# Attention and mixture of experts on one core: batch 0's values ahead of the next keys at the start, and the table filled from another tile

## The chip, the cores and the metric

The kernel runs on one core of a Trainium2 chip. The core has a matrix engine (TensorE, "PE" in the profile), a vector engine (VectorE, "DVE"), an activation engine (ScalarE, "ACT"), a general engine (GpSimd, "POOL") and a sync engine ("SP"), whose queue issues the loads and stores. Each engine works through its own instructions in order and waits on semaphores. The metric is device time in microseconds, lower is better, as the median of several executions.

## The reference

```python
# q, k, v: batch 8, heads 8, sequence 576, head size 64
k_p = k.reshape(B, H, Sp, 8, D).mean(axis=3)      # Sp = 72
v_p = v.reshape(B, H, Sp, 8, D).mean(axis=3)
scores = scale * np.matmul(q, k_p.transpose(0, 1, 3, 2))
attn = np.exp(scores - np.max(scores, axis=-1, keepdims=True))
attn = attn / (np.sum(attn, axis=-1, keepdims=True) + 1e-09)
x = np.matmul(attn, v_p)                          # then (4608 tokens, 512)
# experts: tokens with x @ w_skip > 0 go to the argmax of x @ w_gate
h = np.maximum(xc[mask] @ w1[e], 0.0)
y[mask] = gate_w[mask, None] * (h @ w2[e])
out[do_compute] = xc + y
```

Keys and values are averaged over groups of 8 rows, so that each query sees 72 of them. The 4608 tokens then go through 8 experts with 512 and 1024 columns, each token through one or none.

## The kernel before

`attention` goes over 36 tiles of 128 tokens (line 632, `for t in range(NT)`). A batch is 576 tokens, 4.5 tiles. For one tile the steps are: scores of two halves of the heads (TensorE, line 296), the minima of the negated scores (VectorE, line 303, tile `nm`), eight exponentials (ScalarE, line 310, `e`), six transposes (TensorE, lines 321 and 325) with two copies (ScalarE, lines 322 and 326), the product with the values (TensorE, line 339, two tiles or more later), and the normalisation and store (VectorE and SP, lines 356 to 364). `LAG = 4`: tile t's loop pass does the scores of t, the exponentials of t - 1, the transposes of t - 2 and the values of t - 4. Three PSUM buffers hold score halves, so a half needs the buffer of the half three before it.

A batch's keys are loaded into `stage` (`load_k`, line 187), summed over 8 by VectorE in four groups (line 209, tile `kp`) and written by ScalarE into a block-diagonal tile `kbd` (line 212). A batch's values are loaded into `hlo` or `hhi`, with a small remainder in `vl` (`load_v`, line 215), and summed over 8 (`pool_v`, lines 230 to 232, tiles `vs` and `ls`): on VectorE for batch 0, on POOL for the rest. TensorE transposes the sums (line 255), ScalarE copies them (`vT`), TensorE multiplies them with the gate columns (line 264), ScalarE copies these (`gs`), and two products (lines 273 and 276) put them beside the values in `vbd` and `vl4`.

The order on PE, ACT and DVE is that of the program's text (`manual_schedule`, line 154). It is set by generators that are stepped in the loop: `extra` (line 609) steps the key sums, `sums` (line 627) steps the value sums, and lines 682 to 691 start a batch's values or load the next. SP issues in the order of the text, with at most eight transfers under way before it waits for the one eight back. POOL's order is made by a scheduler that follows the dependencies.

Before the loop (lines 585 to 602) three matmuls on the tile `init` warm TensorE, and the loads go out: keys 0, the queries of tiles 0 and 1, the identity, the queries of tiles 2 and 3, values 0, keys 1, constants. `table` (in memory, 36,864 rows of two numbers) is filled with a marker from `init`, whose memory is later the ring of token tiles, and which is therefore cleared a second time (lines 448 and 449).

Of the kernel before, what the change touches and what calls it, by code (L numbers as in the profile page):

```python
# [26 lines left out]
F32 = mybir.dt.float32  # L27
# [12 lines left out]
NTOK = B * S  # L40
# [66 lines left out]
def emit(tc, q, k, vm, vr, wg, w1, w2, cf, out):  # L107
    nc = tc.nc
    with ExitStack() as top:
# [13 lines left out]
        rows = cp.tile([SLOTS, 256], F32, name="rows")  # L123
# [37 lines left out]
def attention(tc, nc, q, k, vm, vr, cf, w1, w2, whi, wlo, out, c, pay, offs, table, load_constants, near, bufs, late, early, fin):  # L161
    with ExitStack() as ctx:
# [10 lines left out]
        init = early("ring", 128, F)  # L173
        nc.gpsimd.memset(init, NO_TOKEN)
# [12 lines left out]
        def load_k(b, part=0):  # L187
            n = 4 * SP * POOL
            kt = flat(stage)[:, b % 2 * n:b % 2 * n + n].rearrange("p (g k i) -> p g k i", g=4, i=POOL)
            if part:  # L190
                for g in (range(0, 1) if part == 1 else range(1, 4)):
                    nc.sync.dma_start(kt[:, g], k[b, :, g])
            else:
                nc.sync.dma_start(kt, k[b])
            return kt
# [26 lines left out]
        def pool_v(b, vt, vl):  # L222
# [49 lines left out]
            eng = nc.gpsimd if b else nc.vector  # L272
            eng.tensor_tensor(vb.rearrange("p g (h c) -> p g h c", h=2)[:, :, :, HD:VA - 1],
                                    gs[:, 0:72].rearrange("p (g h c) -> p g h c", g=4, h=2),
                                    pair.unsqueeze(3).broadcast_to([128, 4, 2, 9]), ALU.mult)
            eng.tensor_tensor(v4[:n, :, HD:VA - 1], gs[:n, 72:108].rearrange("p (g c) -> p g c", g=4),
# [3 lines left out]
        def load_q(i, part=0, qt=None):  # L280
            s = 128, QG, 4, 128
            qt = qt or (qp.tile(list(s), F32, name="qt") if i % 3 == 2 else early("xlo" if i % 3 else "xhi", *s))
            sl = (slice(None), slice(0, 1), slice(1, QG))[part]
            nc.sync.dma_start(qt[:, sl], q[i, :, sl])
            return qt
# [147 lines left out]
        def near_tokens():  # L433
# [14 lines left out]
            late("ring")  # L448
            nc.gpsimd.memset(bufs["ring"], 0.0)

# [141 lines left out]
        load_q(0, 2, qt[0])  # L592
        qt[1] = load_q(1)
        vt[0] = load_v(0)
        start_k(1)
        load_constants()
# [4 lines left out]
        nc.gpsimd.dma_start(table.rearrange("(p n) t -> p (n t)", p=128), init[:, 0:NE * NTOK * 2 // 128])  # L601
# [7 lines left out]
        def extra(budget):  # L609

            if kcur in kg and t > max(0, 4.5 * kcur - KAHEAD):
                next(kg[kcur], None)
                if kcur == 1:
                    next(kg[kcur], None)
                budget -= 7
            while budget > 0 and routes.step():
                budget -= 1
            if los and budget > 0:
                los.pop(0)[1]()
# [12 lines left out]
        for t in range(NT):  # L632
# [12 lines left out]
            if t > 0:  # L645
                es[t - 1] = exped(*sms.pop(t - 1))
# [30 lines left out]
            if t >= LAG:  # L677
                for _, b in parts(t - LAG):
                    if b in vgen:
                        finish(vgen.pop(b))  # L680
                os_[t - LAG] = values(t - LAG, *pts.pop(t - LAG))
            if nv < B and t >= max(3, 4.5 * nv + LAG - VAHEAD):
                vgen[nv] = pool_v(nv, *vt.pop(nv))
                next(vgen[nv])
                nv += 1
                if 1 < nv < B:
                    vt[nv] = load_v(nv)
            if t == 0:
                start_k(2)
            if t == 1:  # L690
                vt[1] = load_v(1)
# [94 lines left out]
def slots(tc, nc, c, offs, table, near, bufs, out, fin, p, psum):  # L786
# [50 lines left out]
    nc.gpsimd.indirect_dma_start(rows[:, :], None, table.rearrange("(r l) t -> r (l t)", l=128),  # L837
# [27 lines left out]
    rv = rows.rearrange("s (l t) -> s t l", t=2)  # L865
# [407 lines left out]
```

## Time and profile before

| | us |
|---|---|
| median of 3 runs | 561.47 (559.93 to 565.52) |
| the profiled execution | 559.05 |
| its span in the trace | 557.2 |
| mean granted TensorE clock | 0.978 |

The attention loop fills roughly the first 170 us of the span, and the experts the rest. A row of the trace's order of time gives start, duration, engine, line, operation, what it writes and reads, and in brackets the idle time before it and what ended that. In a row for a window the engines' busy times are followed by the granted clock, the busy share of the DMA engines and the GB/s that they moved. A row of transfers ends with the time from issue to landing.

### The profile page before, as it was taken

Reading aid. Unit: us, or ns where it says so; the run is one execution under the profiler, and the core shown is the slowest. Engines: PE = TensorE matmul, PEld = TensorE weight load, DVE = VectorE, ACT = ScalarE, POOL = GpSimd, SP = SyncE. Lnnn points to the kernel's source line nnn. Section 1 sums busy time; section 2 is a strip of 40 time slices with the busy share of each in tenths; the row PEclk is TensorE's granted clock in tenths of the full one; section 3 lists DMA queues with packets and bytes.
Section 4 is the critical chain, followed back from the end, with each engine's and each line's share of the span. In section 5 each row is a group of like instructions: output and inputs, shape, how many; then the busy total and the mean of one; then the engine's idle time right before and its main releaser. Section 6 shows DMA issues by size and latency. Waiting matters only on the chain. (4 is left out here: it accounts for less than half of the span.)

```text
span 557.2 us, 11058 instructions
## 1 busy us (share of the span) xinstructions
PE 509.7 (91%) x3346; PEld 456.0 (82%) x3347; DVE 296.6 (53%) x698; ACT 244.7 (44%) x671; POOL 215.4 (39%) x291
## 2 busy tenths in 40 slices
PE   7489999698898968999999999999999999999994
PEld 5389898587797848797989898998989898989893
DVE  3567777595767732224633563233254557565663
ACT  5459789488882112123422441222144445443441
POOL 3638628468963424120422042323232043304042
PEclk9689999799999999999999999999999999999998
DMA  8958879977992111014331533111243637462200
GB/s 292 383 226 319 293 269 224 332 247 170 285 235 80 23 38 49 22 59 172 115 125 56 169 129 103 57 38 54 75 169 121 244 108 268 157 239 101 95 27 7
DMA packets 33447, 86.03 MB, mean 154 GB/s; under 512 B 7485, under 2 KB 7746, under 8 KB 31488
## 3 DMA queue, kind: packets, MB, share of 16 engines
q1 hardware_dynamic: 25312, 71.62, 39.9%
q0 software_dynamic: 8096, 13.95, 7.7%
q8 instruction: 18, 0.29, 0.3%
q14 instruction: 21, 0.17, 0.1%
HBM read 73.79 MB, written 20.52 MB: 169 GB/s over the span
## 5 line engine op out<-in xcount | busy, mean ns | idle before, releaser
L1070 PE MATMUL psl<-xhi,w1hi 128*128 128x256 f32 (+3 forms) x416 | 122.0, 293 | 5.0 <-PEq L900 3.9
L1071 PE MATMUL psl<-xlo,w1hi 128*128 128x256 f32 (+3 forms) x416 | 121.3, 292 | 0.0
L1072 PE MATMUL psl<-xhi,w1lo 128*128 128x256 f32 (+3 forms) x416 | 121.3, 291 | 0.0
L1126 ACT ACTIVATE hhi<-psl 128x256 fp32r<-128x256 f32 (+4 forms) x104 | 41.9, 403 | 155.2 <-ACTq L900 154.2
L989 POOL DMA_INDIRECT out<-ring,slot x39 | 40.0, 1025 | 179.9 <-POOLq L900 172.5
L1085 PE MATMUL psf<-w2hi,hhi 128*128 128x512 f32 x240 | 96.1, 400 | 2.9 <-PEq L900 2.9
L1086 PE MATMUL psf<-w2lo,hhi 128*128 128x512 f32 x240 | 94.8, 395 | 0.0
L1183 DVE SCALAR_TENSOR_TENSOR hlo<-psl,hhi 128x256 fp32r<-128x256 f32 (+2 forms) x104 | 43.8, 423 | 79.0 <-DVEq L900 78.5
L1070 PEld LDWEIGHTS psl<-xhi,w1hi 128*128 128x128 f32 x416 | 78.1, 188 | 7.0 <-issue 6.4
L1088 PE MATMUL psf<-w2hi,hlo 128*128 128x512 f32 x200 | 79.1, 395 | 0.0
L1071 PEld LDWEIGHTS psl<-xlo,w1hi 128*128 128x128 f32 x416 | 78.2, 188 | 0.5
L1072 PEld LDWEIGHTS psl<-xhi,w1lo 128*128 128x128 f32 x416 | 78.1, 188 | 0.0
L310 ACT ACTIVATE e<-sc,nm 128x72 f32<-128x72 f32 x288 | 64.6, 347 | 11.8 <-DVE nm L303 11.5
L1172 DVE SCALAR_TENSOR_TENSOR ring<-psf,ring 128x512 f32 x25 | 18.8, 750 | 78.8 <-DVEq L900 78.8
L339 PE MATMUL o<-vbd,pT 128*128 128x148 f32 (+1 forms) x304 | 49.7, 300 | 9.8 <-DVE x L363 8.5
L1085 PEld LDWEIGHTS psf<-w2hi,hhi 128*128 128x128 f32 x240 | 45.1, 188 | 13.0 <-issue 3.3
L1086 PEld LDWEIGHTS psf<-w2lo,hhi 128*128 128x128 f32 x240 | 45.1, 188 | 9.7
L339 PEld LDWEIGHTS o<-vbd,pT 128*128 128x128 f32 (+1 forms) x304 | 41.2, 184 | 11.7 <-issue 9.1
L1135 ACT ACTIVATE xhi<-psd 128x512 fp32r<-128x512 f32 x36 | 18.9, 600 | 70.9 <-ACTq L900 70.9
L984 POOL DMA_INDIRECT ring<-out,slot x39 | 43.4, 1114 | 15.0 <-issue 12.5
L1088 PEld LDWEIGHTS psf<-w2hi,hlo 128*128 128x128 f32 x200 | 37.6, 188 | 9.1
L423 POOL DMA_INDIRECT table<-pay,r_di x36 | 35.6, 989 | 23.0 <-DVE rc L358 9.7
(220 smaller groups left out, 859.0 us busy)
## 6 DMA issues: line engine op xcount, KB each, us to landing
stage<-in_w SPq DMA_DIRECT2D x64, 512.0 KB, 4.4
out<-x SPq DMA_DIRECT2D x36, 256.0 KB, 5.7
stage<-in_k SPq DMA_DIRECT2D x7, 1152.0 KB, 8.9
hlo<-in_vm SPq DMA_DIRECT2D x4, 1024.0 KB, 9.8
hhi<-in_vm SPq DMA_DIRECT2D x4, 1024.0 KB, 7.0
xlo<-in_q SPq DMA_DIRECT2D x6, 512.0 KB, 6.6
qt<-in_q SPq DMA_DIRECT2D x6, 512.0 KB, 7.3
xhi<-in_q SPq DMA_DIRECT2D x5, 512.0 KB, 12.6
```

Of the source, the lines that this page charges most:

```text
L310: nc.scalar.activation(e[:, h, :], sc[h // 4][:, h % 4 * SP:(h % 4 + 1) * SP], AF.Exp, bias=nm[:, h:h + 1], scale=-1.0)
L339: nc.tensor.matmul(o_[sl, g * 2 * VA:(g + 1) * 2 * VA], pT[:, 2 * a + g, sl], vbd[b % 3][:, 2 * a + g, :], start=(g == 0), stop=False)
L984: g.indirect_dma_start(ring[:, s % 6, 0:D], None, out, bass.IndirectOffsetOnAxis(ap=slot[:, s:s + 1], axis=0), bounds_check=NTOK - 1, oob_ ...
L989: g.indirect_dma_start(out, bass.IndirectOffsetOnAxis(ap=offsets, axis=0), ring[:, s % 6, 0:D], None, bounds_check=NTOK - 1, oob_is_err=Fa ...
L1070: t.matmul(ps, whi[0][:, k, w], xhi[:, k, xs], start=(k == 0), stop=False)
L1071: t.matmul(ps, whi[0][:, k, w], xlo[:, k, xs], start=False, stop=False)
L1072: last = t.matmul(ps, wlo[0][:, k, w], xhi[:, k, xs], start=False, stop=(k == 3))
L1085: t.matmul(ps, hhi[:, k, sl], whi[1][:, k, :], start=(k == 0), stop=False)
L1086: last = t.matmul(ps, hhi[:, k, sl], wlo[1][:, k, :], start=False, stop=(short and k == 7))
L1088: last = t.matmul(ps, hlo[:, k, sl], whi[1][:, k, :], start=False, stop=(k == 7))
L1126: a.activation(hhi[:, f, xs], psL[f % 3][:, xs], AF.Relu).then_inc(sem["act"], 1)
L1183: m = v.scalar_tensor_tensor(to[:, f], psL[f % 3][:, cs], 0.0, hhi[:, f, cs].bitcast(F32), ALU.max, ALU.subtract)
```

## The change

1. Values 0, the constants and then the queries of tiles 2 and 3 are loaded in this order ahead of keys 1, and keys 1 come in two halves. Values 1 are loaded ahead of keys 2.
2. Batch 0's values are summed from tile 1 on instead of tile 3; the sums of keys 1 begin a tile later (`max(1, ...)` for `max(0, ...)`). At t = 4 the exponentials of tile 3 and the value product of tile 0 come before the scores.
3. The two gate products of batch 0 (lines 273 and 276) go from VectorE to POOL.
4. `rows` gets 128 partitions, holds the marker and fills `table` in three pieces per partition. The ring is cleared at the start, 512 columns of it ahead of the warming matmuls, and no second time.

```diff
-        init = early("ring", 128, F)
-        nc.gpsimd.memset(init, NO_TOKEN)
+        late("ring")
+        init = flat(bufs["ring"])
+        nc.gpsimd.memset(init[:, 0:512], 0.0)
...
+        nc.gpsimd.memset(init[:, 512:], 0.0)
...
-                nc.sync.dma_start(kt, k[b])
+                n = 2 if b == 1 else 4
+                for g in range(0, 4, n):
+                    nc.sync.dma_start(kt[:, g:g + n], k[b, :, g:g + n])
...
-            eng = nc.gpsimd if b else nc.vector
-            eng.tensor_tensor(vb.rearrange(...)
+            nc.gpsimd.tensor_tensor(vb.rearrange(...)
...
-            late("ring")
-            nc.gpsimd.memset(bufs["ring"], 0.0)
...
+        vt[0] = load_v(0)
+        load_constants()
         qt[1] = load_q(1)
-        vt[0] = load_v(0)
         start_k(1)
-        load_constants()
...
-        nc.gpsimd.dma_start(table.rearrange("(p n) t -> p (n t)", p=128), init[:, 0:NE * NTOK * 2 // 128])
+        nc.gpsimd.dma_start(table.rearrange("(p a n) t -> p a (n t)", p=128, a=3),
+                            fin["rows"][:, 0:NE * NTOK * 2 // 384].unsqueeze(1).broadcast_to(...))
...
-            if kcur in kg and t > max(0, 4.5 * kcur - KAHEAD):
+            if kcur in kg and t > max(1, 4.5 * kcur - KAHEAD):
...
+            if t == LAG:
+                es[t - 1] = exped(*sms.pop(t - 1))
+                finish(vgen.pop(0))
+                os_[0] = values(0, *pts.pop(0))
...
-            if t > 0:
+            if t > 0 and t != LAG:
                 es[t - 1] = exped(*sms.pop(t - 1))
...
-            if t >= LAG:
+            if t > LAG:
                 for _, b in parts(t - LAG):
...
-            if nv < B and t >= max(3, 4.5 * nv + LAG - VAHEAD):
+            if nv < B and t >= max(3 if nv else 1, 4.5 * nv + LAG - VAHEAD):
...
             if t == 0:
+                vt[1] = load_v(1)
+            if t == 1:
                 start_k(2)
-            if t == 1:
-                vt[1] = load_v(1)
```

The new text is up to five lines longer, so the same operation has a line number up to five higher after the change (the reduction of line 209 is line 213, the scores of line 296 line 299).

VectorE, from the last minima of tile 1 to the minima of tile 4 (`kp`: key sums of batch 1; `hlo`, `vs`: value sums of batch 0), before:

```order
3 L303 TENSOR_REDUCE nm<-sc 128x4 x4
4 L209 TENSOR_REDUCE kp<-stage 128x72 x2
5 L303 TENSOR_REDUCE nm<-sc 128x4 x2
6 L209 TENSOR_REDUCE kp<-stage 128x72 x2
7 L303 TENSOR_REDUCE nm<-sc 128x4 x2
8 L230 TENSOR_TENSOR hlo<-hlo 128x1024
9 L231 TENSOR_TENSOR hlo<-hlo 128x512
10 L232 TENSOR_TENSOR vs<-hlo 128x256
11 L247 TENSOR_SCALAR vbd_121<-vs,cfs 128x2x64 x4
12 L273 TENSOR_TENSOR vbd_121<-gs,cfs 128x8x9
13 L276 TENSOR_TENSOR vl_124<-gs,cfs 64x4x9
14 L303 TENSOR_REDUCE nm<-sc 128x4 x2
```

and after:

```order
3 L306 TENSOR_REDUCE nm<-sc 128x4 x4
4 L234 TENSOR_TENSOR hlo<-hlo 128x1024
5 L235 TENSOR_TENSOR hlo<-hlo 128x512
6 L236 TENSOR_TENSOR vs<-hlo 128x256
7 L251 TENSOR_SCALAR vbd_121<-vs,cfs 128x2x64 x4
8 L306 TENSOR_REDUCE nm<-sc 128x4 x2
9 L213 TENSOR_REDUCE kp<-stage 128x72 x2
10 L306 TENSOR_REDUCE nm<-sc 128x4 x2
11 L213 TENSOR_REDUCE kp<-stage 128x72 x2
12 L306 TENSOR_REDUCE nm<-sc 128x4 x2
```

The value sums have moved ahead of the minima of tile 2 and of all key sums of batch 1, and the two gate products have left the engine.

TensorE, from the second score half of tile 4 to the first of tile 6 (`sc`: scores; `mps<-cfs`: transposes of summed values, `mps<-wgs`: gate products), before. Here the `mps` rows belong to batch 0:

```order
19 L296 MATMUL sc<-kbd_115,qt 64x144
20 L296 MATMUL sc<-kbd_116,qt 64x144
21 L255 MATMUL mps<-cfs,vs 128x128 x2
22 L256 MATMUL mps<-cfs,ls 64x64
23 L264 MATMUL mps<-wgs,vT 128x36 x2
24 L265 MATMUL mps<-wgs,vT 64x36
25 L339 MATMUL o<-vbd_121,pT 128x148 x2
26 L341 MATMUL o<-vl_124,p_237 128x148
27 L339 MATMUL o<-vbd_121,pT 128x148 x2
28 L341 MATMUL o<-vl_124,p_237 128x148
29 L296 MATMUL sc<-kbd_116,qt 128x144 x2
```

and after, where they belong to batch 1:

```order
28 L299 MATMUL sc<-kbd_115,qt 64x144
29 L299 MATMUL sc<-kbd_116,qt 64x144
30 L259 MATMUL mps<-cfs,vs 128x128 x2
31 L260 MATMUL mps<-cfs,ls 64x64
32 L299 MATMUL sc<-kbd_116,qt 128x144 x2
33 L324 MATMUL pt<-cfs,e 128x128 x4
34 L328 MATMUL pr<-cfs,e 128x128 x2
35 L268 MATMUL mps<-wgs,vT 128x36 x2
36 L269 MATMUL mps<-wgs,vT 64x36
```

Batch 0's rows, with the value product of tile 0, have moved ahead of tile 4's scores, and batch 1's transposes now stand directly behind them, two tiles earlier than before.

The load queue, from the second q load of tiles 0 and 1 on (`hlo` and `hhi`: values, `stage`: keys, `xhi`, `xlo` and `qt`: queries), before:

```order
5 L284 DMA xhi<-in_q 128x512
6 L284 DMA xlo<-in_q 128x1024
7 L218 DMA hlo<-in_vm 128x2048
8 L219 DMA vl<-in_vr 64x512
9 L194 DMA stage<-in_k 128x2304
10 L143 DMA cfs<-in_cf 128x352
11 L144 DMA wgs<-in_wg 128x108
12 L284 DMA qt<-in_q 128x1024
13 L194 DMA stage<-in_k 128x2304
14 L218 DMA hhi<-in_vm 128x2048
```

and after:

```order
5 L287 DMA xhi<-in_q 128x512
6 L222 DMA hlo<-in_vm 128x2048
7 L223 DMA vl<-in_vr 64x512
8 L143 DMA cfs<-in_cf 128x352
9 L144 DMA wgs<-in_wg 128x108
10 L287 DMA xlo<-in_q 128x1024
11 L198 DMA stage<-in_k 128x1152 x2
12 L287 DMA qt<-in_q 128x1024
13 L222 DMA hhi<-in_vm 128x2048
14 L223 DMA vl<-in_vr 64x512
15 L198 DMA stage<-in_k 128x2304
```

The queries of tiles 2 and 3 have gone behind values 0 and the constants, and keys 2 behind values 1.

More of the change, by code (lines that the diff above doesn't have):

```diff
@@ L122, in emit @@
         offs = cp.tile([128, NE], F32, name="offs")
-        rows = cp.tile([SLOTS, 256], F32, name="rows")
+        rows = cp.tile([128, 256], F32, name="rows")
         slot = cp.tile([128, SLOTS], I32, name="slot")
@@ L271, in pool_v @@
             yield
-            eng = nc.gpsimd if b else nc.vector
-            eng.tensor_tensor(vb.rearrange("p g (h c) -> p g h c", h=2)[:, :, :, HD:VA - 1],
+            nc.gpsimd.tensor_tensor(vb.rearrange("p g (h c) -> p g h c", h=2)[:, :, :, HD:VA - 1],
                                     gs[:, 0:72].rearrange("p (g h c) -> p g h c", g=4, h=2),
                                     pair.unsqueeze(3).broadcast_to([128, 4, 2, 9]), ALU.mult)
-            eng.tensor_tensor(v4[:n, :, HD:VA - 1], gs[:n, 72:108].rearrange("p (g c) -> p g c", g=4),
+            nc.gpsimd.tensor_tensor(v4[:n, :, HD:VA - 1], gs[:n, 72:108].rearrange("p (g c) -> p g c", g=4),
                                     left.unsqueeze(2).broadcast_to([n, 4, 9]), ALU.mult)
@@ L600, in attention @@
             nc.gpsimd.tensor_copy(vl4[i][0:4 * KL, :, VA - 1], c["left"])
-        nc.gpsimd.dma_start(table.rearrange("(p n) t -> p (n t)", p=128), init[:, 0:NE * NTOK * 2 // 128])
+        nc.gpsimd.dma_start(table.rearrange("(p a n) t -> p a (n t)", p=128, a=3),
+                            fin["rows"][:, 0:NE * NTOK * 2 // 384].unsqueeze(1).broadcast_to([128, 3, NE * NTOK * 2 // 384]))
         finish(pool_k(0, kt))
@@ L836, in slots @@
     nc.vector.tensor_tensor(coli, col[:, 1:2], col[:, 2:3], ALU.add)
-    nc.gpsimd.indirect_dma_start(rows[:, :], None, table.rearrange("(r l) t -> r (l t)", l=128),
+    nc.gpsimd.indirect_dma_start(rows[0:SLOTS, :], None, table.rearrange("(r l) t -> r (l t)", l=128),
                                  bass.IndirectOffsetOnAxis(ap=coli[0:SLOTS, :], axis=0),
@@ L864, in slots @@
     yield WROWS
-    rv = rows.rearrange("s (l t) -> s t l", t=2)
+    rv = rows[0:SLOTS].rearrange("s (l t) -> s t l", t=2)
     tp = psum.tile([128, 4, 128], F32, name="mps")
```

## The prediction

> **What bounds the kernel now.** I read the page first, for the shares by engine and the granted clock, then who waited for whom in the first 60 us, since that is where the change sits, then the order of time from 10 to 45 us, then the landing of single transfers and the clock in narrow windows.
>
> The page says that TensorE is the engine that fills the span, and that it does so least at the start.
>
> ```profile
> span 557.2 us, 11058 instructions
> PE 509.7 (91%) x3346; PEld 456.0 (82%) x3347; DVE 296.6 (53%) x698; ACT 244.7 (44%) x671; POOL 215.4 (39%) x291
> PEclk9689999799999999999999999999999999999998
> ```
>
> The waits of the first 60 us (engine and line, whom it waited for, us in total, times, longest) show one wait for a load on VectorE, TensorE's largest wait behind it, and one of POOL.
>
> ```profile
> POOL ring L449 <- DMA table<-ring: 7.9, 1, 7.9
> ...
> DVE kp L209 <- DMA stage<-in_k: 6.6, 1, 6.6
> ...
> PE sc L296 <- ACT e L310: 6.4, 1, 6.4
> ```
>
> The order of time (start, duration, engine, line, operation) gives the chain, and the durations that the sum uses. I call the 128-row tiles t0 to t35 and the two score halves of a tile a and b.
>
> ```profile
> 11.05 0.73 PE L296 MATMUL sc<-kbd,xlo 128*128 128x144 f32 x4 [0.46 <-DMA xlo<-in_q]
> 17.68 1.41 DVE L209 TENSOR_REDUCE kp<-stage 128x72 f32<-128x576 f32 x2 [6.60 <-DMA stage<-in_k]
> ...
> 19.49 1.80 ACT L310 ACTIVATE e<-sc,nm 128x72 f32<-128x72 f32 x8 [6.20 <-DVE nm L303]
> ...
> 20.50 1.33 PE L296 MATMUL sc<-kbd,xlo 128*128 128x144 f32 x4 [6.43 <-ACT e L310]
> ...
> 21.87 0.91 ACT L212 ACTIVATE kbd<-kp 64x288 f32<-64x288 f32 x2
> 22.24 1.22 DVE L230 TENSOR_TENSOR hlo<-hlo 128x1024 f32<-128x1024 f32 x1
> ...
> 24.05 1.12 PE L321 MATMUL pt<-cfs,e 128*128 128x128 f32 x4
> ...
> 24.67 0.88 DVE L247 TENSOR_SCALAR vbd<-vs,cfs 128x128 f32<-128x128 f32 x4
> ...
> 24.95 0.64 PE L325 MATMUL pr<-cfs,e 128*128 128x128 f32 x2
> ...
> 25.50 2.76 POOL L230 TENSOR_TENSOR hhi<-hhi 128x256 f32<-128x256 f32 x4 [4.81 <-DMA hhi<-in_vm]
> ...
> 26.68 0.69 PE L255 MATMUL mps<-cfs,vs 128*128 128x128 f32 x2
> ...
> 27.65 0.38 ACT L258 ACTIVATE vT<-mps 128x256 f32<-128x256 f32 x1 [1.58 <-PE mps L256]
> ...
> 28.19 0.64 PE L264 MATMUL mps<-wgs,vT 128*128 128x36 f32 x4 [0.57 <-ACT vT L259]
> ...
> 29.35 0.90 DVE L273 TENSOR_TENSOR vbd<-gs,cfs 128x72 f32<-128x72 f32 x1 [3.80 <-ACT gs L267]
> 30.17 1.13 DVE L276 TENSOR_TENSOR vl<-gs,cfs 64x36 f32<-64x36 f32 x1
> ...
> 31.21 0.31 POOL L232 TENSOR_TENSOR ls<-vl 64x64 f32<-64x64 f32 x1
> 31.23 0.81 DVE L303 TENSOR_REDUCE nm<-sc 128x4 f32<-128x288 f32 x2
> ...
> 33.55 1.10 PE L296 MATMUL sc<-kbd,qt 128*128 128x144 f32 x4
> ```
>
> VectorE is through with t1 at 11.08 (the wait of 6.60 counted back from 17.68) and stands before batch 1's key sums, because in its order they come before t2's minima. ScalarE cannot exponentiate t2, so t3b has no PSUM buffer, and TensorE stands until 20.50. Batch 0's value sums come after that, 22.24 to 25.55, then a wait of 3.80 us, then the two gate-column products, and only at 31.23 t4's minima. t5a starts at 33.55.
>
> **The change, part by part.** My milestone is t8a. From there on both kernels issue the same work in the same order, so its shift, S, is what is left at the end.
>
> ```profile
> 44.83 0.65 PE L296 MATMUL sc<-kbd,xlo 128*128 128x144 f32 x4
> ...
> 48.52 0.76 PE L296 MATMUL sc<-kbd,xlo 128*128 128x144 f32 x4
> ...
> 51.77 0.65 PE L296 MATMUL sc<-kbd,qt 128*128 128x144 f32 x4
> ```
>
> A plain tile takes 51.77 - 48.52 = 3.25 us of a full TensorE. From t5a to t8a stand three tiles, batch 1's value transposes (about 0.5) and its gate products (about 0.7): 33.55 + 3 x 3.25 + 1.2 = 44.5, against 44.83 seen, so nothing else binds there. The change takes the transposes out of this stretch (now ahead of t5a): t8a follows t5a by 3 x 3.25 + 0.7 = 10.4 us.
>
> (1) Landings. These are issues of the queue and, below them, the landing times of the same transfers (us from issue, last number).
>
> ```profile
> 4.49 0.43 SPq L218 DMA_DIRECT2D hlo<-in_vm  x1
> hlo<-in_vm SPq DMA_DIRECT2D x1, 1024.0 KB, 9.8
> ...
> 7.84 0.74 SPq L284 DMA_DIRECT2D qt<-in_q  x1
> qt<-in_q SPq DMA_DIRECT2D x1, 512.0 KB, 11.6
> ...
> 9.22 0.33 SPq L194 DMA_DIRECT2D stage<-in_k  x1
> stage<-in_k SPq DMA_DIRECT2D x1, 1152.0 KB, 13.0
> ```
>
> Landings came in order of issue: q of t2/t3 (xlo) at 10.9, values 0 (hlo) at 14.3, keys 1 at 17.7, q of t4/t5 (qt) at 19.4, keys 2 at 22.2, values 1 (hhi) at 25.5. Values took 14.3 - 10.9 = 3.4 us. A q load of 512 KB took 19.4 - 17.7 = 1.7 us, so the loads ahead of the second q were done at about 9.2; values 0, put there, land at 12.6. Their remainder and the constants (358 KB, about 1 us at the same rate) now also precede the second q, which then lands at 15.3 instead of 10.9. Keys 1, in two halves, complete where they did, near 18, since the bytes ahead are the same. Values 1 take the place of keys 2: 22.3. Keys 2 then come near 25.5.
>
> (2) VectorE. The 3.3 us of value sums (22.24 to 25.55) go to 12.6 to 15.9, inside the 6.6 us wait: free. The two gate products go to POOL, which does the same shapes for the other batches in 0.31 us for the larger, and is idle there (it waits for values 1): free.
>
> ```profile
> L273 POOL TENSOR_TENSOR vbd<-gs,cfs x7: 298/307/328, 43.2 to 164.0; 128x72 f32<-128x72 f32 x7
> ```
>
> (3) TensorE now waits for the second q, 10.6 to 15.3, instead of standing 14.07 to 20.50. Its clock decides the next prices.
>
> ```profile
> 17.25:17.50 0.25, 0.00 (x0) 0.00 (x0) 0.00 (x0) 0.00 (x0) 0.17 (x2) 0.79 1.10 419
> ...
> 27.50:28.00 0.50, 0.11 (x1) 0.00 (x0) 0.00 (x0) 0.35 (x2) 0.50 (x2) 0.87 0.88 363
> ```
>
> The granted clock (third number from the right) fell 3.4 us after the last matmul and came back at 27.6, 7.1 us after work began again. I take the same here: half clock from 15.3 to 22.4. Half-clock prices: 1.3 for the scores of half a tile, 1.55 for six transposes (24.05 to 25.59), 0.95 for the value transposes (26.68 to 27.65), 0.55 for their copies (to 28.19), 1.15 for gate products and copies (to 29.35). At full clock the scores take 0.65; by that ratio and the fixed part of each I put the six transposes at 0.95 and the value transposes at 0.55. The chain: t2a 16.6, transposes t0 18.15, t2b 19.45, value transposes 20.4, copies 20.95, gate products and copies 22.1. ScalarE's exponentials of t2 end at 23.9; TensorE meanwhile does t3a and the transposes of t1, to 23.85, and t3b, on the buffer that t2a held, to 24.5. t3's second minimum (half of 0.81) 24.95, the last two key sums (1.41) 26.4. ScalarE has exponentiated t3 from 25.0 to 26.8, then writes the keys, 0.91: 27.7. t4a 28.35, transposes t2 29.3, t4b 30.0, batch 1's value transposes 30.55, t5a. I add 0.5 us for hand-overs: t5a 31.05, t8a 41.45, S = 44.83 - 41.45 = 3.4 us.
>
> The bounds: with a full clock throughout t4b ends at 28.5 and S = 4.9; at half clock until t5a it starts at about 34.5 and S = 0. I take 3.4, by the row above, which is this kernel's own recovery.
>
> The Trainium skill, "TensorE: Matmul & The Clock Gate", Part 1, says that the clock halves after an idle window of about 3.4 us and is released after one busy window of that length. That speaks against the new order too, whose gap is still longer than a window; the fall in the trace agrees, the recovery was slower than one window. By the page's release the clock would be back by 18.7 to 22.1, S about 4 and the time 557.5.
>
> (4) New wait. Batch 1's value transposes stand in TensorE's order behind t4b, two tiles earlier than before, and everything of t5 stands behind them. POOL's sums take 6.0 us after the landing (25.50 to 31.52): 28.3, against 30.0 when TensorE comes. Hidden, with 1.7 us to spare.
>
> (5) POOL. Clearing the whole ring early and filling the table from the smaller tile take away POOL's wait of 7.9 us; the sums behind it are first used by the value transposes at 26.68, which follow VectorE's values at 25.55, so the wait cost nothing. The table's fill is the same 288 KB in three times as many pieces; at a q load's rate that is 1.0 us of the queue, ahead of the second q or behind it, so S may change by 1.0 either way. I take nothing.
>
> Does S last? The stretch after t8a is paced by TensorE, and the queue had run dry in between (last number, GB/s).
>
> ```profile
> 34.00:36.00 2.00, 2.00 (x16) 2.00 (x16) 1.55 (x5) 0.81 (x3) 0.00 (x0) 0.89 0.02 7
> ...
> 101.94 1.33 PE L339 MATMUL o<-vbd,pT 128*128 128x148 f32 x4 [5.59 <-DVE x L363]
> ```
>
> Sum: the profiled execution took 559.05 us (span 557.2 and 1.85 around it), so 555.65 for it. The median of the runs shown is 2.4 us above it, 561.47, and I forecast against that: 561.47 - 3.4 = 558.1.
>
> **The rivals.** (B) Nothing is left at the end. The second row above is a stall behind output stores in a loaded queue; if that stage is paced by the queue alone, an earlier start only waits longer there: 561.5. For it: the 5.59 us themselves. Against it: the queue moved 7 GB/s at 34 to 36 us, so its backlog begins anew and moves with the compute.
> (C) More than my sum: the shifted loads lose that stall as well, 558.1 - 5.6 = 552.5. For it: the stall hangs on which transfers meet. Against it: their order is unchanged.
> (D) Slower: values 1 land late, and TensorE stands at the transposes of (4). It begins to cost at a landing of 24.0, eats all of S at 27.4, and passes 1% at 33.0. If they share the queue with keys 2, the next q and values 2 and land with these at about 29.8, the time is 561.47 + 2.4 = 563.9. For it: POOL waited 4.81 us for these values before, until 25.50, the last of the first loads to come. Against it: landings kept the order of issue.
> That the change does nothing at all is not to be expected, as VectorE's and TensorE's orders do differ at t2; its time would be that of (B).
>
> **How the numbers follow.** My case, S from 2 to 5 (556.5 to 559.5), 0.64; (B) 0.14; (C) 0.12; (D) 0.10. About 1% (5.6 us) is what a measurement of this kernel can tell from no change. Faster by more than that needs (C) or my case beyond its upper bound, 0.12 + 0.04 = 0.16; slower by more is the far end of (D), 0.04; within 1% the rest, 0.80. The range leaves out most of (C) and the far half of (D): 554.5 to 562.8.
>
> **What would show it.** Right: VectorE's sums of hlo at about 12.5 to 15; TensorE's gap ending near 15.3 by the q load; t5a between 29 and 32, t8a between 40 and 42.5; the same distance later at 101.94's stall. Wrong: a POOL wait ahead of the hhi sums that ends after 24, with the value transposes idle before them; a half clock that lasts past 25; or t8a early and the end not.

## The result and the profile after

| | us |
|---|---|
| before, median of 4 runs (range) | 563.3 (559.93 to 565.52) |
| after, median of 4 runs (range) | 556.33 (554.45 to 559.07) |
| ratio | 0.9895, 95% interval 0.9853 to 0.9937 |
| profiled execution after, its span | 556.37, 554.6 |

The two medians lie 7.0 us apart; by the ratio the change gains 5.9 us of 563 (3.5 to 8.3 by the interval). The same kernel, timed twice more in the experiments below, gave 0.9921 (0.9882 to 0.9959) and 0.9895 (0.9857 to 0.9932). It is a gain of about 1%.

The page of the profile after (span; busy time of TensorE, VectorE, ScalarE and GpSimd; granted clock in tenths over 40 slices):

```profile
span 554.6 us, 11051 instructions
PE 513.1 (93%) x3346; PEld 460.4 (83%) x3347; DVE 298.7 (54%) x696; ACT 244.7 (44%) x671; POOL 215.7 (39%) x293
PEclk8799999999899978999999999999999999999997
```

TensorE's busy time has risen by 3.4 us while the span has shrunk: more of its work ran at half clock, 22.6 us over the whole span against 14.0 before (added up from windows of 0.25 us). This is not so at the start, where it is less (6.6 us in the first 42 us, 9.8 before). What is new lies at 143 to 146 us and between 197 and 211 us (slices 11, 15 and 16). The waits of the first 60 us after (engine and line, whom it waited for: us in total, times, longest):

```profile
POOL hhi L234 <- DMA hhi<-in_vm: 5.6, 2, 4.7
...
PE sc L299 <- DMA xlo<-in_q: 3.1, 1, 3.1
...
PE sc L299 <- ACT kbd L216: 1.6, 2, 1.4
```

VectorE's wait of 6.6 us for keys 1 and TensorE's 6.4 us behind it are gone. TensorE waits 3.1 us for the second q instead. The order of time after (start, duration, engine, line, operation, idle time ahead and its releaser):

```profile
12.25 1.22 DVE L234 TENSOR_TENSOR hlo<-hlo 128x1024 f32<-128x1024 f32 x1
...
14.98 1.30 PE L299 MATMUL sc<-kbd,xlo 128*128 128x144 f32 x4 [3.14 <-DMA xlo<-in_q]
16.07 1.06 PE L324 MATMUL pt<-cfs,e 128*128 128x128 f32 x4
...
18.88 0.31 PE L260 MATMUL mps<-cfs,ls 64*64 64x64 f32 x1
...
20.33 0.30 PE L269 MATMUL mps<-wgs,vT 64*64 64x36 f32 x2
...
21.86 0.76 PE L299 MATMUL sc<-kbd,xlo 128*128 128x144 f32 x4
...
22.39 2.78 POOL L234 TENSOR_TENSOR hhi<-hhi 128x256 f32<-128x256 f32 x4 [0.90 <-DMA hhi<-in_vm]
...
24.88 0.94 ACT L216 ACTIVATE kbd<-kp 64x288 f32<-64x288 f32 x2
...
25.87 0.70 PE L299 MATMUL sc<-kbd,qt 128*64 128x144 f32 x6 [1.36 <-ACT kbd L216]
...
28.23 0.44 PE L259 MATMUL mps<-cfs,vs 128*128 128x128 f32 x2 [0.20 <-POOL vs L236]
...
28.77 0.76 PE L299 MATMUL sc<-kbd,qt 128*128 128x144 f32 x4
...
39.51 0.65 PE L299 MATMUL sc<-kbd,xlo 128*128 128x144 f32 x4
...
95.20 1.33 PE L342 MATMUL o<-vbd,pT 128*128 128x148 f32 x4 [4.16 <-DVE x L366]
```

The milestone t8a comes at 39.51, so S = 44.83 - 39.51 = 5.3 us, where 3.4 was forecast. All values of S below are counted from this one trace of the kernel before. The stall in mid-attention ends at 95.20 instead of 101.94, 6.7 us earlier, of which 1.4 is a shorter stall. The granted clock in narrow windows after (third number from the right):

```profile
9.50:10.00 0.50, 0.50 (x4) 0.50 (x4) 0.04 (x1) 0.50 (x4) 0.00 (x0) 0.50 0.84 344
...
19.50:20.00 0.50, 0.24 (x2) 0.24 (x3) 0.50 (x2) 0.21 (x2) 0.00 (x0) 0.77 0.94 389
20.00:20.25 0.25, 0.25 (x4) 0.25 (x3) 0.25 (x1) 0.00 (x0) 0.00 (x0) 1.00 1.36 442
```

The clock was at a half from 9.5 to 19.7, so t3's scores (20.56 and 21.86) and all that follows up to 30 us ran at the whole clock.

### The profile page after: what moved, and what is told of

It is laid out like the page before. It is cut to its first block, busy times and chain, and to the rows that moved or that the text cites. A ratio compares the mean times of both kernels' runs of the same rounds, so it can differ in the third digit from the quotient of the medians.

```text
span 554.6 us, 11051 instructions
## 1 busy us (share of the span) xinstructions
PE 513.1 (93%) x3346; PEld 460.4 (83%) x3347; DVE 298.7 (54%) x696; ACT 244.7 (44%) x671; POOL 215.7 (39%) x293
## 5 line engine op out<-in xcount | busy, mean ns | idle before, releaser
L1075 PE MATMUL psl<-xhi,w1hi 128*128 128x256 f32 (+3 forms) x416 | 123.4, 297 | 5.1 <-PEq L905 3.8
L1076 PE MATMUL psl<-xlo,w1hi 128*128 128x256 f32 (+3 forms) x416 | 122.6, 295 | 0.0
L1075 PEld LDWEIGHTS psl<-xhi,w1hi 128*128 128x128 f32 x416 | 79.5, 191 | 7.1 <-issue 6.5
L1076 PEld LDWEIGHTS psl<-xlo,w1hi 128*128 128x128 f32 x416 | 79.6, 191 | 0.5
L1077 PEld LDWEIGHTS psl<-xhi,w1lo 128*128 128x128 f32 x416 | 79.4, 191 | 0.0
L1177 DVE SCALAR_TENSOR_TENSOR ring<-psf,ring 128x512 f32 x25 | 18.7, 749 | 78.7 <-DVEq L905 78.7
L989 POOL DMA_INDIRECT ring<-out,slot x39 | 45.0, 1154 | 15.6 <-issue 13.4
L426 POOL DMA_INDIRECT table<-pay,r_di x36 | 35.7, 990 | 22.3 <-DVE rc L361 9.9
```

The source lines that it names most:

```text
L989: g.indirect_dma_start(ring[:, s % 6, 0:D], None, out, bass.IndirectOffsetOnAxis(ap=slot[:, s:s + 1], axis=0), bounds_check=NTOK - 1, oob_ ...
L1075: t.matmul(ps, whi[0][:, k, w], xhi[:, k, xs], start=(k == 0), stop=False)
L1076: t.matmul(ps, whi[0][:, k, w], xlo[:, k, xs], start=False, stop=False)
L1077: last = t.matmul(ps, wlo[0][:, k, w], xhi[:, k, xs], start=False, stop=(k == 3))
```

## The experiments

The runs came in three groups on three chips, each beside the kernel before, and ratios are to that. The second group is fill_gap, gates_on_vector, q_ahead and fill_exit; the third begins with changed_beside. In the first and third group the kernel before took 563.29 and 563.30 us, in the second 580.11. There only ratios and the first 45 us of the traces are comparable with the rest.

| run | t8a, us | median, us | ratio (95%) |
|---|---|---|---|
| changed_again | 40.96 | 558.17 | 0.9921 (0.9882 to 0.9959) |
| ring_table_only | 44.61 | 563.06 | 1.0011 (0.9973 to 1.0050) |
| old_ring_table | 39.18 | 557.64 | 0.9899 (0.9859 to 0.9939) |
| keys2_first | 42.20 | 561.22 | 0.9959 (0.9913 to 1.0006) |
| fill_gap | 38.84 | 574.19 | 0.9907 (0.9873 to 0.9941) |
| gates_on_vector | 39.49 | 574.61 | 0.9926 (0.9900 to 0.9953) |
| q_ahead | 39.91 | 573.02 | 0.9885 (0.9835 to 0.9936) |
| fill_exit | 40.14 | 572.33 | 0.9864 (0.9811 to 0.9916) |
| changed_beside | 40.57 | 557.75 | 0.9895 (0.9857 to 0.9932) |
| fill_gap_late1 | 39.53 | 557.97 | 0.9913 (0.9881 to 0.9945) |
| q_ahead2 | 39.83 | 556.97 | 0.9885 (0.9840 to 0.9930) |
| q_ahead2_fill | 38.70 | 557.38 | 0.9889 (0.9839 to 0.9939) |

### The changed kernel again, and its parts

**changed_again**: no edit.

> The changed kernel once more, unaltered. In its first profile t5a started at 28.77 us and t8a at 39.51, 5.3 us ahead of the kernel before, and the span ended 2.6 us ahead. My account of the start (value sums inside the wait for the keys) expects t8a within 1 us of 39.5 again and a ratio of 0.987 to 0.994. The rival, that the first profile's start was lucky with the phase of the clock, expects t8a anywhere from 39 to 42 and a ratio nearer 0.995.

The clock fell at 13.3 and came back only at 26.9. Windows of 3.4 us of that stretch and behind it (PE's busy time is the second number, the granted clock the third from the right):

```profile
20.00:23.40 3.40, 3.40 (x16) 3.25 (x17) 0.84 (x2) 1.98 (x11) 1.64 (x4) 0.50 1.04 326
23.40:26.80 3.40, 3.40 (x16) 3.40 (x15) 1.78 (x3) 2.82 (x11) 3.40 (x5) 0.50 1.01 413
26.80:30.20 3.40, 3.40 (x29) 2.37 (x28) 0.87 (x3) 1.60 (x4) 2.12 (x5) 0.98 1.01 310
```

t8a came at 40.96, S = 3.9. This is further from 39.5 than the account allowed and inside the rival's range, while the ratio of 0.9921 fits the account. So the size of S belongs to the execution, not to the kernel alone: with a half clock that ended 7.2 us later, t8a came 1.45 us later.

**ring_table_only**: the kernel before with part 4 of the change alone.

```diff
-        init = early("ring", 128, F)
-        nc.gpsimd.memset(init, NO_TOKEN)
+        late("ring")
+        init = flat(bufs["ring"])
+        nc.gpsimd.memset(init[:, 0:512], 0.0)
...
-        nc.gpsimd.dma_start(table.rearrange("(p n) t -> p (n t)", p=128), init[:, 0:NE * NTOK * 2 // 128])
+        nc.gpsimd.dma_start(table.rearrange("(p a n) t -> p a (n t)", p=128, a=3),
...
```

> The kernel before with only the ring cleared at once and the table filled from rows. My account gives nothing for it by itself: t8a at 44 to 45.5, ratio 0.997 to 1.003, since batch 0's remainder sums are used only after VectorE's values at about 26. The rival, that POOL's wait of 7.9 us was what held the start, expects t8a 2 to 4 us earlier and a ratio near 0.994.

Ratio 1.0011, t8a within 0.22 us of the kernel before. The title's second half is worth nothing by itself that ten runs show; their interval leaves room for 1.5 us. GpSimd's wait of 7.9 us is gone without a gain. The start did not stay the same, though. TensorE's order of time and the last window at half clock of ring_table_only:

```profile
19.48 1.33 PE L298 MATMUL sc<-kbd,xlo 128*128 128x144 f32 x4 [5.41 <-ACT e L312]
...
31.75:35.17 3.42, 3.42 (x16) 3.41 (x16) 1.57 (x5) 1.32 (x6) 0.00 (x0) 0.50 0.21 65
```

Keys 1 were there 1.0 us earlier (16.66 against 17.68), and TensorE's stall ended 1.0 us earlier. Then the clock stayed at a half from 18.1 to 35.2, where the trace before had it whole again from 27.6 to 31.0, and the lead was gone by t8a. Whether the earlier landing comes from the table's fill, which is issued at 6.66 us here and at 4.64 before, or from the execution, one trace of each does not tell.

**old_ring_table**: the changed kernel with part 4 undone.

```diff
-        late("ring")
-        init = flat(bufs["ring"])
-        nc.gpsimd.memset(init[:, 0:512], 0.0)
+        init = early("ring", 128, F)
+        nc.gpsimd.memset(init, NO_TOKEN)
...
+            late("ring")
+            nc.gpsimd.memset(bufs["ring"], 0.0)
```

> The changed kernel with the ring and table as before: table filled from the ring's memory, which is cleared a second time after that. The prediction's step 5 priced this part at nothing: t8a at 39.5. The trace of the changed kernel speaks against that: the remainder's sums on POOL ended at 17.8 and TensorE waited for them at 18.87. With POOL held to about 16 by the fill and the second clearing, they would end at 19.5 to 20.5, and t8a would come 1 to 2.5 us later, at 40.5 to 42, the ratio to the kernel before near 0.994.

This expectation, made after the result, was that the old wait would now be in the way, since the value sums had moved ahead. It missed. GpSimd's order of time in old_ring_table:

```profile
12.52 2.67 POOL L450 MEMSET ring<- 128x3096 f32 x1 [7.15 <-DMA table<-ring]
...
18.45 0.31 POOL L234 TENSOR_TENSOR ls<-vl 64x64 f32<-64x64 f32 x1
```

The wait of 7.15 us is there, and the small value sum ends at 18.76, about 1 us later than after the change (17.8). TensorE, which stands for q first, reaches that transpose at 18.88 in the trace after, so the 1 us is not missed. t8a (39.18) and the ratio (0.9899) are no worse than with part 4, which stays worth nothing here, as step (5) of the prediction had it.

**keys2_first**: the changed kernel with keys 2 loaded ahead of values 1, as before the change.

```diff
             if t == 0:
-                vt[1] = load_v(1)
-            if t == 1:
                 start_k(2)
+            if t == 1:
+                vt[1] = load_v(1)
```

> The changed kernel with keys 2 loaded ahead of values 1, as before the change. By the prediction's step 4 values 1 then land near 25.5, POOL's sums end near 31.5, TensorE stands at batch 1's value transposes ahead of t5, and t5a starts near 32.2, t8a near 42.7: S falls from 5.3 to 2, ratio 0.995 to 0.998. The rival, that landings do not keep the order of issue and the new wait is hidden in either order, expects t8a at 39.5 and the ratio of the changed kernel.

TensorE's order of time in keys2_first:

```profile
30.92 0.44 PE L259 MATMUL mps<-cfs,vs 128*128 128x128 f32 x2 [2.82 <-POOL vs L236]
...
42.20 0.65 PE L299 MATMUL sc<-kbd,xlo 128*128 128x144 f32 x4
```

The new wait of step (4) is real. With values 1 at 25.1, where they land behind keys 2, GpSimd's sums end near 30.9 and TensorE stands 2.82 us at the transposes; S falls to 2.6 and the gain with it (ratio 0.9959). Up to t4b this trace runs like the first one after the change (27.38 and 27.31), so the 2.7 us at t8a are the price of this order. The medians on this chip lie about 3 us apart, but the intervals of the two ratios overlap. The order of these two loads in the change carries some 2 to 3 us of its gain.

### What sets the size of S

**fill_gap**: the changed kernel with work put into TensorE's wait for q.

```diff
+            if t == 2:
+                for _ in range(5):
+                    nc.tensor.matmul(o[:, 0, 0:256], ident, flat(kbd[0])[:, 0:256], start=True, stop=True)
```

> The changed kernel with five idle-filling multiplications (128 columns by 256, fp32, into an accumulator tile that is not in use) put ahead of t2's scores, in TensorE's wait for the second q load; the output is unchanged. Theory that S hangs on the length of the half clock: if the clock is still whole when they start, they keep it so past t2, t8a comes at 38 to 39.5 us and the median lies about 1 us under the changed kernel's; if it has already been halved by then, the fillers end behind the landing of q and delay t2 by up to 1.5 us, t8a at 40.5 to 41. Rival, that the landing of q and the key chain alone set t8a: t8a stays within 0.5 us of 39.5 whatever the clock rows show.

TensorE's order of time in fill_gap:

```profile
14.53 0.73 PE L299 MATMUL sc<-kbd,xlo 128*128 128x144 f32 x4 [1.70 <-DMA xlo<-in_q]
...
25.30 0.71 PE L299 MATMUL sc<-kbd,qt 128*64 128x144 f32 x8
...
27.55 0.44 PE L259 MATMUL mps<-cfs,vs 128*128 128x128 f32 x2 [1.54 <-POOL vs L236]
...
38.84 0.65 PE L299 MATMUL sc<-kbd,xlo 128*128 128x144 f32 x4
```

The five fillers ran from 10.51 to 12.8, and the clock stayed whole from 10 to 30 us. t4b ended at 26.0, 2.0 us earlier than in the first trace of the changed kernel (28.0), and then TensorE stood 1.54 us at batch 1's value transposes. t8a gained only 0.7: it lies in the theory's range, and the ratio of 0.9907 does not tell this version from the changed kernel. So a faster clock ahead of this point is paid back to the landing of values 1: the two limits, the chain of keys and GpSimd's sums, lie within 2 us of each other.

**gates_on_vector**: the changed kernel with part 3 undone.

```diff
-            nc.gpsimd.tensor_tensor(vb.rearrange(...)
+            (nc.gpsimd if b else nc.vector).tensor_tensor(vb.rearrange(...)
...
```

> The changed kernel with batch 0's two gate products back on VectorE. The prediction put them down as free on GpSimd; on VectorE they wait for the gate copies and stand ahead of t3's or t4's minima and the key sums. Theory: what the move to GpSimd saves is that wait, so t4a and t8a come 0.5 to 2 us later here (t8a 40 to 43 by the phase of the clock), the median 0.5 to 2 us above the changed kernel's. Rival: the products are as free on VectorE, which idles there, and t8a stays at 39.5 to 41.

VectorE's order of time in gates_on_vector:

```profile
21.08 0.23 DVE L276 TENSOR_TENSOR vbd<-gs,cfs 128x72 f32<-128x72 f32 x1 [0.60 <-ACT gs L271]
21.23 0.18 DVE L279 TENSOR_TENSOR vl<-gs,cfs 64x36 f32<-64x36 f32 x1
```

The rival holds: the two products take 0.33 us and lie ahead of minima that were not ready. t8a is 39.49. Both homes of these products are free. Before the change they took 0.90 and 1.13 us on VectorE, while GpSimd was summing (25.50 to 31.52); here GpSimd stood idle from 18.35 until its sums of values 1 at 22.35. This fits what the Trainium skill, "SBUF — State Buffer", says of the port pair that the two engines share, in the section "SBUF: two separate sides": one of the two, GpSimd or an operation of VectorE with two inputs from SBUF, holds it for a whole instruction while the other waits. No run here was made to show that this is the cause.

**q_ahead**: the changed kernel with the second q ahead of values 0 again.

```diff
-SUMS = [1, 2, 4]
+SUMS = [1, 4, 4]
...
+        qt[1] = load_q(1)
         vt[0] = load_v(0)
         load_constants()
-        qt[1] = load_q(1)
...
-            if kcur in kg and t > max(1, 4.5 * kcur - KAHEAD):
+            if kcur in kg and t > max(2, 4.5 * kcur - KAHEAD):
...
-            if nv < B and t >= max(3 if nv else 1, 4.5 * nv + LAG - VAHEAD):
+            if nv < B and t >= max(3 if nv else 2, 4.5 * nv + LAG - VAHEAD):
```

The two loads after tile 0 and tile 1 are also exchanged, as in keys2_first.

> A version meant to beat both: the second q load is issued ahead of batch 0's values (it follows them in the changed kernel), batch 1's value transposes and key sums one tile later, the keys of batch 2 ahead of batch 1's values. Theory that what is left of the stall is TensorE's wait for the second q (landing 15.0): q lands near 11, as in the kernel before, values 0 near 14.5, TensorE does not stand, t4a comes near 22 and t8a at 35.5 to 37, S 8 to 9 us and a ratio of 0.982 to 0.990 against the kernel before. Rival: the key sums of batch 1 (landing near 18) or batch 1's values (near 25.5) take its place; then t8a is 39 or later and the ratio 0.990 or above.

TensorE's order of time in q_ahead:

```profile
14.52 0.76 PE L299 MATMUL sc<-kbd,xlo 128*128 128x144 f32 x4 [0.19 <-ACT e L313]
...
19.27 0.24 PE L260 MATMUL mps<-cfs,ls 64*64 64x64 f32 x1 [1.92 <-POOL ls L236]
...
25.48 1.23 PE L299 MATMUL sc<-kbd,qt 128*64 128x144 f32 x8
```

q was there in time: t2 and t3 were scored by 15.3, 7 us earlier than after the change (22.6). All of that was lost again by t4a, whose keys come behind another chain: GpSimd's copies of the constants delayed the sum of the small value tile, and ScalarE, in its order, stood behind the copies of that transpose before it could exponentiate t3 and write the keys (written by 24.3). TensorE came to t4a only at 25.48, behind tile 0's value product, which ran at half clock from 22.2 on: the clock was halved again from 20.0 to 26.8. t8a 39.9: the rival, though not by the landing that it named. The ratio agrees with the changed kernel's.

**q_ahead2** and **q_ahead2_fill**: both have the edits of q_ahead; in q_ahead2 GpSimd's copies of constants and the columns of ones are written behind the value sums of batch 0; q_ahead2_fill adds fillers.

```diff
-        load_constants()
+        constants = load_constants()
...
                 next(vgen[nv])
+                if nv == 0:
+                    for i in range(3):
+                        for hh in range(2):
+                            nc.gpsimd.tensor_copy(vbd[i][:, :, (hh + 1) * VA - 1], c["pair"][:, :, hh])
+                        nc.gpsimd.tensor_copy(vl4[i][0:4 * KL, :, VA - 1], c["left"])
+                    constants()
```

```diff
+            if b == 0:
+                fill(3)
             for j in range(2):
                 nc.tensor.transpose(tp[:, j, :], vs[:, j * 128:j * 128 + 128], ident)
...
+            if b == 0:
+                fill(3)
             for j in range(2):
                 nc.tensor.matmul(gp[:, j * 36:j * 36 + 36], vT[:, j, :], wgs[:, j * 36:j * 36 + 36], start=True, stop=True)
...
                 finish(vgen.pop(0))
+                fill(6)
```

> The version with the second q load ahead, in which GpSimd's copies of the constants and the columns of ones (16.46 to 18.91 there) no longer stand ahead of the sum of the small value tile, for which TensorE, ScalarE and so the keys of batch 1 waited. Theory: that sum is done near 16.8 instead of 19.2, t4a comes near 23 instead of 25.5, and t8a near 37.5, a ratio of 0.982 to 0.988. Rival: the clock is halved in the gap of TensorE from 16 to 21 and gives it back, t8a at 39 or later.

> The same with twelve fillers (three ahead of batch 0's value transposes, three ahead of its gate products, six ahead of batch 1's first scores); the output is unchanged. Theory: the clock stays whole from 10 us on, t8a comes 0.5 to 2 us earlier than without them (36 to 37), a ratio of 0.980 to 0.987. Rival: each filler that lasts beyond its gap delays the chain (up to 0.7, 0.7 and 1.4 us), and t8a is the same or later.

In q_ahead2 the edit did not do what it said: on GpSimd the scheduler sets the order, and the sum of the small tile stayed behind ten of the copies (first and last row of the stretch):

```profile
16.55 0.79 POOL L693 COPY vbd<-cfs 128x4 f32<-128x4 f32 x2
...
18.76 0.31 POOL L240 TENSOR_TENSOR ls<-vl 64x64 f32<-64x64 f32 x1
```

t4a came at 25.34 and t8a at 39.83; the theory was not put to the test. In q_ahead2_fill the clock stayed whole, but its last fillers outlasted their gap. TensorE's order of time there:

```profile
20.21 2.86 PE L610 MATMUL o<-kbd,cfs 128*128 128x256 f32 x12
...
24.86 0.71 PE L307 MATMUL sc<-kbd,qt 128*64 128x144 f32 x8
...
38.70 0.65 PE L307 MATMUL sc<-kbd,xlo 128*128 128x144 f32 x4
```

GpSimd's gate products ended at 21.1, so tile 0's value product could have begun 2 us earlier than 23.18. t8a came at 38.70, the earliest of all, but only 0.14 us ahead of fill_gap's. The keys were written by 23.07, so a version without the last six fillers would, by an estimate from these rows, reach t4a near 23; that was not tried.

**fill_gap_late1**: fill_gap with `SUMS = [1, 4, 4]` for `[1, 2, 4]`, which puts batch 1's value transposes a tile later.

> The changed kernel with the five fillers ahead of t2's scores and batch 1's value transposes one tile later; the output is unchanged. With the fillers alone the clock stayed whole and TensorE then stood 1.54 us at these transposes, waiting for GpSimd's sums (step 4's wait, with the roles turned). Theory: taken out of the way it gives those 1.5 us: t5a near 26.1 us, t8a near 37.3, and a median 1 to 2 us below the changed kernel's. Rival: another wait (t5's or t6's q load, the next key sums) takes the same time, t8a at 38.5 or later.

TensorE's order of time in fill_gap_late1:

```profile
15.08 1.10 PE L299 MATMUL sc<-kbd,xlo 128*128 128x144 f32 x4 [2.00 <-DVE vs L236]
...
39.53 0.65 PE L299 MATMUL sc<-kbd,xlo 128*128 128x144 f32 x4
```

Here the same fillers did not hold the clock: it fell near 15.3 (mean 0.82 from 14 to 16, 0.50 from 16 to 18), after a wait of 2.0 us (the row names VectorE's sum, which these scores do not read; the second q, issued at 7.06, landed 7.9 us later, at 15.0), and t4a came where the changed kernel has it. The transposes no longer stood in the way, but nothing was there to be gained. Whether the two together bring t8a to 37 stays open.

### Where the lead goes later

In the first trace after, the lead of 6.8 us at ScalarE's last copy of attention (204.10 before, 197.33 after) had shrunk to 4.0 at the first expert activation (211.76, 207.78), with a half clock from 204.1 to 210.9 that the trace before does not have.

**fill_exit**: the changed kernel with twelve fillers at that place.

```diff
...
+        def last(i):
+            fill(2)
+            tx(ring[:, i], i)()
-        follow = [lambda: [tx(ring[:, i], i)() for i in range(3)]]
+        follow = [lambda: [last(i) for i in range(3)]]
...
+        fill(6)
         return held
```

> The changed kernel with twelve idle-filling multiplications (128 columns by 256, fp32) where attention ends: two ahead of each of the last three transposes of x, six behind them; the output is unchanged. In the profiled execution of the changed kernel about 4 us of its lead were lost there, with the granted clock at a half from 197.5 to 200.5 and from 203.7 to 211. Theory that the phase of the clock decides this: the clock stays whole there, the first expert activation comes no later than 205.5, and the median is 1 to 3 us under the changed kernel's with a smaller spread. Rival: the entry is paced by the routing on the other engines, and the fillers only stand in the way: same or up to 2 us slower.

The clock in windows of fill_exit:

```profile
222.00:224.00 2.00, 0.02 (x1) 0.04 (x1) 0.48 (x1) 0.00 (x0) 0.00 (x0) 1.00 0.00 0
224.00:226.00 2.00, 2.00 (x12) 2.00 (x13) 0.00 (x0) 0.00 (x0) 1.74 (x3) 0.69 0.06 13
```

The fillers kept the clock whole up to the wait of 2.4 us ahead of the first expert product; just behind that wait it was halved all the same. The first activation came at 226.36, 10.1 us after the last copy of attention, against 9.0 us in fill_gap, whose exit is that of the changed kernel. The theory missed: its clock did not stay whole, and the way from the last copy to the first activation, 10.5 and 8.7 us in two traces of the changed kernel, got no shorter that one could tell. The ratio of 0.9864 (0.9811 to 0.9916) is the lowest of all, but its interval, from four runs, overlaps those of the changed kernel, so whether the fillers help on the whole is not settled.

**changed_beside**: the changed kernel once more, beside the third group.

> The changed kernel unaltered, beside the versions of this group. Theory (the gain of the whole run is the shift S at t8a, which the phase of the clock moves between 3.9 and 5.6 us): a ratio of 0.990 to 0.993 to the kernel before, t8a at 39 to 41. Rival, that what lies behind attention adds to it: a ratio under 0.988.

This run and ring_table_only (the old order of the loads) lie close to the medians of their kernels, and make the best pair for following the lead. Order of time of ring_table_only:

```profile
44.61 0.65 PE L298 MATMUL sc<-kbd,xlo 128*128 128x144 f32 x4
...
103.49 0.83 PE L341 MATMUL o<-vbd,pT 128*128 128x148 f32 x2 [7.38 <-DVE x L365]
...
207.31 0.60 ACT L487 ACTIVATE xhi<-mps 128x512 fp32r<-128x512 f32 x1 [1.48 <-PE mps L485]
215.95 0.39 ACT L1126 ACTIVATE hhi<-psl 128x256 fp32r<-128x256 f32 x1 [8.04 <-ACTq L900]
```

and of changed_beside:

```profile
40.57 0.65 PE L299 MATMUL sc<-kbd,xlo 128*128 128x144 f32 x4
...
99.71 1.33 PE L342 MATMUL o<-vbd,pT 128*128 128x148 f32 x4 [7.63 <-DVE x L366]
...
202.92 0.60 ACT L488 ACTIVATE xhi<-mps 128x512 fp32r<-128x512 f32 x1 [1.43 <-PE mps L486]
211.66 0.38 ACT L1131 ACTIVATE hhi<-psl 128x256 fp32r<-128x256 f32 x1 [8.14 <-ACTq L905]
```

The lead is 4.0 us at t8a, 3.8 behind the stall of mid-attention, 4.4 at the exit of attention, 4.3 at the first expert activation and 4.6 in the span (561.2 and 556.6). It stays between 3.8 and 4.6 us: in this pair the gain of the whole run is about S. The ratio of 0.9895 lies between the theory's range and the rival's. The first pair of traces is less plain: its lead was 5.3 us at t8a, 6.8 where attention ends, 4.0 at the first expert activation and 2.6 in the span.

## Why the prediction was right

The forecast was 558.1 us, within 554.5 and 562.8; the first measurement gave 556.33, and the twenty timed runs of the changed kernel together have a median of 558.1. Against the kernel before, though, the gain was larger than said: 3.4 us forecast, 4.4 to 5.9 in the three comparisons. Two errors hide each other, the base (561.47 from three runs, 563.3 from four) and S, so that the time was met to 0.1 us is luck.

**(1) Landings: right.** Values 0 were there by 12.25 (forecast 12.6), the second q at 14.98 (15.3), values 1 at 22.39 (22.3). That keys 1 come in two halves had no run of its own; VectorE came to their sums at 18.93 without a wait, behind t2's minima.

**(2) VectorE: right.** The value sums ran from 12.25 to 16.0, in time in which VectorE had no other work. The gate products cost nothing on GpSimd; gates_on_vector shows that they would have cost nothing on VectorE either.

**(3) The chain: right in mechanism, S too small.** The mis-sized term is step (3)'s sum to t8a = 41.45, which measured 39.51 in the first trace. The difference of 1.94 adds up stage by stage:

| until | forecast | measured | earlier by | added |
|---|---|---|---|---|
| q lands | 15.3 | 14.98 | 0.32 | 0.32 |
| value transposes end | 20.4 | 19.19 | 1.21 | 0.89 |
| gate products and copies end | 22.1 | 20.98 | 1.12 | -0.09 |
| t3b ends | 24.5 | 22.62 | 1.88 | 0.76 |
| keys written | 27.7 | 25.82 | 1.88 | 0.00 |
| t4b ends | 30.0 | 28.02 | 1.98 | 0.10 |
| t5a starts | 31.05 | 28.77 | 2.28 | 0.30 |
| t8a | 41.45 | 39.51 | 1.94 | -0.34 |

The largest part, 0.89, is not the clock: at half clock from end to end, t2's scores, the transposes of t0 and the value transposes took 4.2 us where the forecast added up 5.1. It summed the durations of groups (1.3 + 1.55 + 1.3 + 0.95), while such groups overlap in the trace: t2a is listed with 1.30 us from 14.98, and the next group starts at 16.07, 1.09 later. Start to start is the price. The next part, 0.76, is TensorE's way to the end of t3b: the forecast let t3a begin behind the copies of the gate products, at 22.1 and at half clock until 22.4; it began at 20.56, 0.4 us before these copies ended, at the whole clock. The 0.5 us for hand-overs were mostly not needed: from the end of t4b to t5a it took 0.75, where the forecast had 1.05 with them.

Two readings of the forecast were wrong without harm in this trace. The 1.15 us for gate products and copies are called a half-clock price, but their rows (28.19 to 29.35) lie behind the return of the clock at 27.6; at half clock they took 1.77 in changed_again (19.81 to 21.58). In the first trace the clock came back just ahead of them. And the 7.1 us from the start of work to the whole clock in the trace before were taken as the kernel's own: here it was 4.8 (to 19.7), in changed_again 11.9 (to 26.9) and in changed_beside 9.5 (to 24.2), with S = 5.3, 3.9 and 4.3. The trace before also had a second half clock that the prediction did not look at, and that is part of S:

```profile
31.04:34.46 3.42, 3.11 (x13) 3.05 (x13) 2.25 (x8) 1.80 (x8) 1.09 (x3) 0.50 0.60 230
```

The bounds lay too late as well. "A full clock throughout" was put at t4b ending at 28.5 and S = 4.9; fill_gap had t4b at 26.0, and the first trace an S of 5.3 with a half clock in it. "Half clock until t5a", put at t5a near 34.5 and S = 0, did not occur; in changed_again the half clock lasted until 0.4 us before t4a (27.30), t5a came at 30.21, and S was 3.9. Both bounds carry the same summed durations.

By the rule of the Trainium skill, "TensorE: Matmul & The Clock Gate", Part 1, which the prediction weighed (release after one busy window of about 3.4 us; the table there says at least one), the clock would be back by 18.7 to 22.1. The first trace agrees (19.7); the two repeats took longer, and in changed_again a stretch of 3.4 us with TensorE busy throughout (20.00 to 23.40) passed at half clock.

**(4) The new wait: right.** In the trace after, GpSimd's value sums end at 28.17 (the small remainder at 28.45, forecast 28.3) and TensorE waits for them 0.20 us at the transposes; it was to be hidden with 1.7 us to spare, and all of this margin went since TensorE came 2 us earlier. keys2_first (2.82 us) and fill_gap (1.54 us) show the wait at work, at the place that the prediction named.

**(5) Ring and table: right in what it is worth.** ring_table_only moves neither t8a nor the time (1.0011), and undoing this part gives 0.9899. The 1.0 us that step (5) left open may be the 1.0 us by which keys 1 landed earlier in ring_table_only; there the clock took it back.

**The rivals.** (B), nothing left, falls: the intervals of all three ratios of the changed kernel end below 1, and the lead of changed_beside over ring_table_only is about the same from t8a to the end. (C), the stall of mid-attention lost as well, falls: it was 4.16 us in one trace after, 6.98 and 7.63 in the others, against 5.59 and 7.38 with the old loads. (D), values 1 late, did not happen, but keys2_first shows what it would have taken: a landing at 25.1 brings a wait of 2.82 us and leaves S at 2.6. By the prediction's own sum, a cost from 24.0 on, such a landing would have cost 1.1; it cost more because TensorE came to the transposes 2 us earlier than forecast.

"Within 1%" was given 0.80 and "faster by more" 0.16. The three ratios, 0.9895, 0.9921 and 0.9895, lie at that line; they can't tell which side it is.

**A better version?** Three ways around the wait for q (q_ahead, q_ahead2, q_ahead2_fill) removed it, and gave 0.9885, 0.9885 and 0.9889: not to be told from the change itself. Each time t8a stayed between 38.7 and 39.9, because the next wait or chain was close behind: the sum of the small value tile, tile 0's value product, the fillers themselves.

## What to carry to other kernels

When a load's order is changed so that one engine's wait disappears, list the chains that end just behind it (here: q, the keys of the next batch through three engines, and the next values through GpSimd); the change can gain no more than the distance to the second-latest of them, and three attempts to pass it gained nothing measurable here. Price a chain by the starts of its groups in the order of time, not by adding their listed durations. Where the granted clock changes within a run, look at the same kernel's spread over executions first (1.45 us at t8a in three traces here), before single traces are compared.

## What the hardware showed that was not expected

The half clock around the same idle gap lasted 10.2 us (9.5 to 19.7), 13.7 us (13.3 to 26.9) and 10.2 us (13.9 to 24.2) in three executions of one kernel. These lengths are multiples of 3.41 us, and that holds in general here: in the fourteen traces of this case, windows of 0.4 us over the first 240 us show 66 stretches of half clock, 30 of 3.41 us, 26 of 6.83, 8 of 10.24, and one each of 13.66 and 17.07 (ring_table_only). Within one trace all rises and falls lie on one grid with this step, to 0.02 us, and the grid lies differently in each execution.

A whole step without work is not needed for a fall. In the first trace after, the fall at 9.5 came before the long wait, after waits of 0.54 and three times about 0.24 us ahead of the first score groups. In changed_again and changed_beside it came 2.4 and 2.9 us after the last matmul. Windows of changed_beside:

```profile
17.40:20.80 3.40, 2.83 (x13) 2.18 (x11) 1.78 (x3) 0.83 (x4) 0.52 (x1) 0.50 1.05 392
20.80:24.20 3.40, 3.40 (x16) 3.37 (x16) 0.46 (x1) 3.12 (x14) 2.96 (x6) 0.50 0.98 376
```

The clock came back at 24.2: one window with 3.40 us of work sufficed here; 2.83 us did not. In changed_again a window of 3.40 us did not suffice and a second did; in the first trace after, the clock came back at the end of a window with 2.89 us of work. What exactly releases it is left open. Another surprise is the chip of the second group, on which the kernel before took 580.11 us instead of 563.3, while the lead of the changed kernel's versions over it was the same within the intervals.
